# A new order table with its PSUM banks and load gates written out, for sliding-window attention followed by a squared-ReLU FFN

## The chip, the cores and the metric

The kernel runs on one core of one Trainium2 chip. The metric is the device time in microseconds (us) of one execution. Besides, one execution is profiled, and the profile's span is the time from its first to its last instruction.

## What is computed

For four batches of eight heads, 768 tokens and a head dimension of 64, each query sees the 96 latest keys and the first eight keys, with a bias that falls with distance. The heads are then put side by side into 3072 tokens of 512 features, and an FFN with a squared ReLU follows.

```python
def _attn_ref(q, k, v, n_global, n_local):
    scores = scale * np.matmul(q, k.transpose(0, 1, 3, 2))
    is_global = pos[None, :] < int(n_global)                  # 8
    is_local = (rel >= 0) & (rel < int(n_local))              # 96
    dist = np.where(is_global & ~is_local, float(n_local), np.abs(rel))
    scores = np.where(is_global | is_local, scores - slopes * dist, -1e9)
    a = softmax(scores)
    return np.matmul(a, v)

def _moe_ref(x, w_in, w_out):              # x: 3072 x 512
    h = np.maximum(x @ w_in, 0.0)          # 512 -> 2048
    return h * h @ w_out                   # 2048 -> 512
```

## The kernel before

The 3072 tokens are cut into eight halves of 384 tokens (half a batch each), numbered 0 to 7; in the code a half is `x`, its number `x.hb`. A half goes through these stages.

Loads: POOL's queue brings q, k and v as 128-row tiles into the staging buffers `sq`, `sk` (one each) and `v` (`list_loads`, L472). The four chunks of w_in (L534) and of w_out (L541) go through the same queue.

Turns: for the first halves, PE transposes sq and sk; from half 3 on, `turn_by_dma` (L647) has SP issue one DMA transpose for k and one for q. `fix` copies the key blocks that stand before a block into `kb`, with the global keys in front, and `values` does the same for `vb`.

Attention: PE makes scores `sp` (L691), ScalarE takes the exponential `ex` (L704), VectorE multiplies by a mask that holds the bias, `phat` (L711, L728), PE multiplies with v and a column of ones, `av` (L752), and `norm` on VectorE divides, a reciprocal `rec` (L760) and a product `tm` (L762). From half 2 on SP transposes `tm` by DMA into `xt` (`to_x_by_dma`, L777).

FFN: `xt` times w_in gives `hps` in PSUM, either in plain products (L797) or in mixed ones (L900), a scheme of fewer products over sums of blocks: `x_mix` holds four sums of quarters of xt (L878), `in_mix` and `w_mix` sums of weights. A mixed product's partial results are held back by a copy (`kept`, L336 on ScalarE or L338 on VectorE) and added later (`hr`, L958). Relu (L822, L824, L966, L968, L981, L983) and square (L836, L838, L998, L1000) give `h`; each of them may run on ScalarE or on VectorE. The second layer (`yps`, L1052 and L1138) mixes likewise: `mixed` (L1103) are sums of h, and partial results go out through `y` (L336, L338, L1200). The output leaves by SP (L1068, L1223).

What sets the order: the program first lists all jobs, PE's as `p` with a number, loads as `l`, and everything else in one list. A table of words, `ORDER`, then gives the order in which they are issued; the letter of a word is the engine (`a` ScalarE, `d` VectorE, `g` POOL, `s` SP, and `l` POOL's loads), so a word with another letter moves a job from one engine to another. In each engine instructions run in the order issued.

`Plan.run` walks the table and simulates a cost model at the same time. From it come two things: which PSUM banks a PE job takes (`idle_banks`, the ones idle longest), and how many filler matmuls (`warm`) a job of the opening issues. A wait between DMAs that data does not ask for is added by `behind(dma, first)`: the first `sk` load of a half stands behind both turns of the half before.

Of the kernel before, what the change touches and what calls it, by code (L numbers as in the profile page):

```python
# [41 lines left out]
AFTER = [0, 0, 0, 0, 0, 0, 0, 0]  # L42
# [10 lines left out]
ORDER = """d1 g2 a4 p0 a6 s8 d12 a0 s10 d17 l3 d13 l1 a18 a16 a19 l2 d21 d20 a27 l5 a26 d14 a22 d15 d3 a28 d5  # L53
p10 l4 a25 d9 p5 a30 d146 l0 a24 p1 a11 p2 d7 l6 a23 p3 l10 a32 d31 a33 d34 p6 l9 a29 d36 p7 a39 p11
d35 l7 p8 a46 p4 d43 p9 a41 l8 d37 p13 d44 a40 p12 d45 a47 l11 p14 d38 p16 a42 p15 d48 l13 p17 d51
a49 p19 p24 a52 l12 d55 p20 d64 p22 a50 p23 d58 l14 a53 p34 d56 p30 a60 p25 d71 p28 l16 p21 a81 d59
p26 d57 a82 l18 p27 d69 d67 p31 a65 d68 p18 a61 p29 l15 d72 p36 p32 a54 d70 p35 l19 a86 d66 p33 a73
d85 p39 d62 p40 l17 a74 a77 d76 p37 l21 d91 a78 p41 l20 d79 d63 p38 d83 l23 a101 d75 d84 p45 l22 a89
a87 d96 p44 l27 p47 a92 d80 p48 d107 a97 l29 d111 p46 a98 p52 l28 p43 a93 d110 p53 p42 d105 l30 d119
p55 d120 p50 l24 p59 a122 a88 d90 d99 a102 p51 l25 d106 a103 d94 p49 a116 a128 d108 p67 d100 a129  # L60
d95 a117 d112 p57 a104 p65 d125 p54 p58 d121 d189 p63 p61 p62 a132 d126 a109 p60 a114 d135 d118 a113
d115 p56 a127 d205 d191 a133 p74 a130 p72 a169 d138 p73 a165 d131 p77 d123 a166 p69 a167 p75 d156
d147 a157 p70 p71 d134 a158 p82 d159 l34 a162 d168 p81 a163 d186 l26 a170 p83 a142 p68 l31 d174 a139
d160 d149 p84 l35 a184 a164 d208 p64 a187 d124 l33 d161 a171 d148 a144 p85 l32 d272 a143 d206 p88
d207 l36 p89 d201 p79 d151 p86 a198 a178 d204 p91 d152 a195 a199 d188 p76 d202 a136 d150 p87 a172
d200 a179 p90 a196 d180 a193 p80 d153 a209 p78 s194 l37 p66 d155 a175 d203 a137 p95 d210 p92 a176
d223 a173 p94 d197 s224 l38 a185 d177 p100 a211 l39 d236 a181 s216 p93 a140 d237 p96 a182 p103 d238
s217 p97 d183 a244 a240 d221 a141 p102 d219 a222 d154 p106 s220 d213 d225 p98 p104 d239 s226 p99
d227 d228 p105 a234 d214 s229 d145 a218 d243 p101 l44 d245 d246 p107 l43 s215 d212 a241 d190 p109
l40 p110 p108 p111 a255 d192 l42 a251 p112 a256 d258 l45 a248 d257 p113 l41 a249 d230 d232 a252 p118  # L70
d259 p114 a273 d253 s260 l46 p116 d254 p115 a261 p120 d231 d250 l47 a262 p122 a264 p124 l48 s235
d280 p123 a265 d263 p131 a268 d233 a283 p127 d281 p126 a288 p132 d285 a269 p134 d295 s328 a287 p129
d270 a286 p119 a291 p142 d266 a293 p140 d296 s329 d314 p130 a311 p135 d267 a299 p128 d315 a292 p137
d274 a312 p136 d300 s242 p121 a305 s282 d327 a302 p125 a306 d289 p138 s275 a284 d303 p141 a307 d301
d304 a276 p117 d294 s290 a313 d308 p133 a271 l50 p139 d330 a278 p143 d297 a309 l56 p145 d279 a316
s298 p146 d310 p147 l53 a317 p144 d405 a334 l51 d322 p148 a326 a337 d323 l52 p149 a335 d443 d340
a331 l49 p151 d324 a341 p150 a332 d336 p152 l54 a342 d318 d325 p157 a348 p153 a343 d333 a345 d344
p159 p156 a346 d320 d319 a354 d407 p158 a356 p161 d321 a338 p172 d355 a359 p154 d349 p162 d377 a351
p169 p163 d360 a372 s378 l57 p164 d363 p167 a361 p166 d365 p171 d347 a368 p177 s408 a369 p160 d339
p165 a364 p170 a362 d357 p178 s409 l55 d373 a386 p175 a366 p173 a387 d382 p180 a367 p174 d376 p182  # L80
d374 p176 a379 s247 d383 p155 d380 s277 a384 s358 p179 d391 a385 p181 d395 a375 p168 s381 d353 d410
a393 p183 l58 a352 p184 d388 a370 a397 d394 l65 s396 p185 a392 d389 a399 d371 l62 p187 a398 d390
p188 p186 a419 l59 p189 d411 a415 a423 d412 l63 p190 a420 d426 a416 p191 d422 l73 a424 d414 a417
p192 l61 d421 a428 d425 p193 p194 p196 a432 l60 d413 a427 d418 a429 p198 p195 a436 d406 a444 d401
a433 p200 d492 p199 d402 a437 d447 p207 a430 p210 d435 a457 p204 s448 d445 p215 a462 p211 d453 p202
s350 d463 s446 p197 d439 a451 p203 d403 a464 p218 d496 d404 p206 a442 d441 d505 a475 d493 p205 a465
d438 p208 s507 p219 a455 d434 p213 a476 p201 d468 s508 a454 d431 a458 p223 p222 a472 d497 p214 a484
d469 d452 p217 a449 p212 s400 d470 a474 p209 d482 a456 p220 p227 d459 a477 s483 d466 p224 a500 p216
d495 a478 s467 l64 p221 d498 a471 p241 d479 a486 p225 l70 p229 a509 d488 d494 l66 p226 a489 d473
p228 a511 d490 a539 l69 d480 p231 d481 p233 l72 p230 a513 d501 d487 a519 l67 d460 p234 a520 d499  # L90
a512 l71 s440 p248 d521 a485 s506 d503 p235 l68 a514 d502 d522 a546 d510 p247 a461 d491 p236 s523
l74 d524 p237 a545 p232 d515 p239 a525 d531 a516 p246 d504 a517 p256 d544 p245 a536 p270 a528 d561
s537 d543 p240 a529 p249 d518 a538 p267 a547 d530 p251 a580 p255 d550 p252 a526 s595 p258 d559 a562
p243 a551 p266 d527 p238 a585 d578 s450 a553 p253 a565 d591 p254 s579 d541 a535 d554 p261 a557 p257
d532 s560 a568 p268 a558 d533 p242 a582 d555 s596 d563 a552 p260 d534 p250 a581 p269 d548 p264 p244
a567 a586 d574 p263 d542 a564 p259 d572 p262 a540 a583 p265 d556 p272 a575 s573 a597 d566 p271 d600
s549 d569 p277 d598 a576 d584 a599 p273 d570 a577 p274 d571 p275 p276 a601 d613 a608 d615 s614 l75
p278 a602 s593 d589 d616 a609 p279 a619 d617 s594 a604 p283 d587 a620 s592 d603 a611 a605 p281 d618
a631 p280 p282 a624 d588 p286 d606 a628 a625 p284 d634 a629 p287 d610 p292 a636 p288 d607 a632 d627
a635 d686 p294 a621 p301 d630 a646 p291 d637 d643 p299 d657 a641 p314 d626 a622 p290 d680 p285 d640  # L100
p307 s681 a633 p305 d623 p300 a665 p295 d655 s642 p293 s612 d647 d590 p296 d668 a644 p298 a656 d648
p309 a658 p289 d649 p308 a670 d654 p297 p304 d638 a651 p311 d652 s639 a663 p312 p306 d669 p317 d687
s653 p310 d688 a690 p302 d676 p316 p320 a684 s677 a650 p303 a685 d674 p328 p319 d671 a662 d666 a697
a672 p313 d659 p315 d696 p331 a675 d682 p318 a660 d691 d667 d678 a719 p333 a661 p332 d689 p321 d692
a664 d683 p335 d695 a716 p352 d698 d705 s699 p347 d693 s645 p334 d742 a752 p322 d723 a722 d673 p337
p339 d679 p336 d706 p338 d700 d720 p324 d721 d728 p329 a725 d753 a724 p343 a710 d729 p341 a726 d701
s711 p342 a717 p340 d736 p323 d694 a737 d734 p344 a738 d702 p345 d709 p325 d703 a740 d708 d707 p351
a712 d731 p353 a730 p326 d727 d704 p346 d750 p348 d713 a741 p327 d732 a733 p349 d714 p357 d746 a715
a754 d735 p330 d743 a755 d739 p354 d751 d764 p350 d744 a756 p356 d718 a748 s757 d747 a745 d749 p355
d760 p362 a758 d761 p358 d765 s759 d763 p368 a770 d779 a768 d767 p364 d762 d766 p359 d769 d775 p360  # L110
d776 d786 a783 p365 d790 d780 d781 p366 a787 d777 p367 a771 a788 p371 d789 d772 d782 s773 p361 d778
d794 p369 s795 d774 p370 d791 p363 d792 s793 p372 a784 p373 d796 s785 s797 a798 a799"""


class Op:
    EARLY = {"ACT": 0.035, "DVE": 0.045}
    LATE = {"ACT": 0.1, "DVE": 0.07}

    def __init__(self, costs, emit, needs, rank=0, lag=0.0, move=None):
        self.emit, self.rank, self.lag, self.move = emit, rank, lag, move  # L120
        self.needs = [n for n in needs if n is not None]
        self.costs = {e: c - self.EARLY.get(e, 0.0) for e, c in costs.items()}
        self.done, self.bufs = None, []
        self.wait = 0.0
        self.takes, self.users, self.rows, self.follows = 0, [], False, []


class Buffer:

    def __init__(self, tag, count):  # L130
        self.tag, self.count, self.users, self.taken = tag, count, [], False
# [7 lines left out]
class Plan:  # L139
# [5 lines left out]
    HOP = 0.08  # L145
    ENTER = 0.19
# [4 lines left out]
    def __init__(self, warm_from, warm_until):  # L151
        self.warm_from, self.warm_until = warm_from, warm_until
        self.queues = {"PE": [], "LOAD": []}
        self.rest = []
        self.free = {e: 0.75 for e in ("ACT", "DVE", "POOL", "SP")}
# [54 lines left out]
    def ready(self, op):  # L210
        t = self.free_at(op)
        if t is None:
            return None
# [1465 lines left out]
```

## Time and profile before

| | before |
|---|---|
| three runs, us | 200.9, 202.91, 202.87 |
| median, us | 202.87 |
| span of the profiled execution, us | 200.3 |
| PE busy, us | 193.0 (96%) |
| VectorE (DVE) busy, us | 178.9 (89%) |
| ScalarE (ACT) busy, us | 155.9 (78%) |
| POOL busy, us | 66.7 (33%) |

The profiled execution's own time is its span of 200.3 us and what lies around it; the nearest of the three runs is 200.9. Engines are named PE (TensorE), PEld (its weight loads), DVE, ACT, POOL (GpSimd) and SP (SyncE, which only issues DMAs here). In a list of waits the last three numbers are microseconds in total, how often, and the longest.

### The profile page before, as it was taken

The numbers are of one execution on the slowest core, as the hardware profiler recorded it, in microseconds if no ns is written. First come the engines' busy times: TensorE is split into PE (matmuls) and PEld (weight loads), VectorE is DVE, ScalarE is ACT, GpSimd is POOL, SyncE is SP. The second block draws the span as 40 slices with busy tenths as digits, with TensorE's granted clock in tenths as the row PEclk, the third lists the DMA queues.
The fourth block names the chain that finished last, engine by engine and source line by source line (L and its number), as shares of the span: only waits on it lengthen the run. The fifth ranks groups of instructions, "written<-read, shape, count | busy, mean of one in ns | idle before, by whom it ended". The sixth has DMA issues, their size and how long they took to land.

```text
span 200.3 us, 5912 instructions
## 1 busy us (share of the span) xinstructions
PE 193.0 (96%) x2346; PEld 161.3 (81%) x2346; DVE 178.9 (89%) x457; ACT 155.9 (78%) x335; POOL 66.7 (33%) x82
## 2 busy tenths in 40 slices
PE   7798999999999899999999999999999999999994
PEld 2685899766897587779878798899888988899993
DVE  7688698899999799989999999999989979998881
ACT  5999676898946889988999798989996669457411
POOL 8996564087108602920095019400000000000000
PEclk9999999999999999999999999999999999999999
DMA  5999999999999999999999989995230330210214
GB/s 154 180 150 197 187 181 173 209 192 154 176 203 74 141 206 219 120 115 99 221 133 147 155 203 144 166 246 111 53 114 3 124 61 3 105 56 0 108 52 157
DMA packets 106987, 27.52 MB, mean 137 GB/s; under 512 B 97104, under 2 KB 104016, under 8 KB 106960
## 3 DMA queue, kind: packets, MB, share of 16 engines
q0 software_dynamic: 74944, 13.11, 93.3%
q1 hardware_dynamic: 30816, 13.45, 30.9%
q10 hardware_dynamic: 1200, 0.59, 1.1%
q8 instruction: 18, 0.29, 0.6%
q14 instruction: 9, 0.07, 0.1%
HBM read 27.26 MB, written 6.29 MB: 167 GB/s over the span
## 4 chain that ended last, share of the span: by engine, by line
PE 72%; DVE 12%; DMA 7%; POOL 3%; ACT 2%; issue 1%; DVEq 0%; POOLq 0%
PE yps L1138 28%; PE hps L797 17%; PE hps L900 17%; DMA w_in_sb<-in_moe_w_in_dram 4%; PE sp L691 3%; PE av L752 3%; DMA xt<-tm 3%; PE yps L1052 2%; DVE phat L728 2%; POOL w_mix L472 2%; DVE tm L762 2%; POOL v L472 1%; ACT ex L704 1%; DVE hr L958 1%; DVE mixed L1103 1%
## 5 line engine op out<-in xcount | busy, mean ns | idle before, releaser
L797 PE MATMUL hps<-xt,w_in_sb 128*128 128x384 f16 (+2 forms) x336 | 45.1, 280 | 0.2 <-DMA w_in_sb<-in_moe_w_in_dram 0.2
L704 ACT ACTIVATE ex<-sp 128x512 f16<-128x512 f32 x66 | 36.4, 632 | 2.6 <-PE sp L691 2.5
L1138 PEld LDWEIGHTS <-h 128*128 128x128 f16 x376 | 34.3, 98 | 5.1 <-DVE h L838 0.2
L797 PEld LDWEIGHTS <-w_in_sb 128*128 128x128 f16 x336 | 28.1, 98 | 7.9 <-DMA w_in_sb<-in_moe_w_in_dram 0.7
L336 ACT COPY y<-yps 128x256 f32<-128x256 f32 (+2 forms) x42 | 15.5, 389 | 17.5 <-PE yps L1138 17.3
L1138 PEld LDWEIGHTS <-mixed 128*128 128x128 f16 x272 | 25.1, 98 | 3.7 <-DVE mixed L1103 0.6
L958 DVE TENSOR_TENSOR hr<-hps,kept 128x384 f16<-128x384 f32 x49 | 25.6, 551 | 2.2 <-ACT h L998 1.1
L472 POOL DMA_DIRECT2D sq<-in_q_dram x19 | 17.2, 907 | 29.7 <-DMA q<-sq 21.6
L336 ACT COPY kept<-hps 128x384 f32<-128x384 f32 x45 | 21.1, 490 | 7.4 <-PE hps L900 4.9
L822 ACT ACTIVATE hr<-hps 128x384 f16<-128x384 f32 (+1 forms) x44 | 22.2, 530 | 4.9 <-PE hps L797 4.8
L472 POOL DMA_DIRECT2D sk<-in_k_dram x19 | 17.1, 901 | 25.3 <-DMA q<-sq 13.6
L900 PEld LDWEIGHTS <-in_mix 128*128 128x128 f16 x272 | 23.0, 98 | 2.3 <-DVE x_mix L878 0.6
L900 PE MATMUL hps<-x_mix,in_mix 128*128 128x192 f16 x204 | 23.4, 246 | 0.3 <-ACT ex L704 0.3
L1138 PE MATMUL yps<-w_out_sb,h 128*128 128x256 f16 (+1 forms) x184 | 22.5, 268 | 0.1
L1138 PE MATMUL yps<-w_mix,mixed 128*128 128x256 f16 (+1 forms) x184 | 22.4, 268 | 0.1
L1138 PE MATMUL yps<-w_mix,h 128*128 128x256 f16 (+1 forms) x192 | 22.4, 264 | 0.0
L472 POOL DMA_DIRECT2D v<-in_v_dram x24 | 21.5, 908 | 2.6 <-DMA w_mix<-in_q_dram 0.9
L728 DVE TENSOR_TENSOR phat<-ex,mask 128x1024 f16<-128x1024 f16 (+1 forms) x36 | 20.7, 598 | 0.0
L900 PEld LDWEIGHTS <-w_in_sb 128*128 128x128 f16 x204 | 17.4, 98 | 2.1 <-issue 0.7
L900 PE MATMUL hps<-xt,w_in_sb 128*128 128x192 f16 x136 | 16.1, 246 | 0.5 <-DMA xt<-tm 0.5
L998 ACT ACTIVATE h<-hr 128x768 f16<-128x768 f16 x19 | 15.9, 853 | 0.4 <-DVE hr L968 0.3
L836 ACT ACTIVATE h<-hr 128x512 f16<-128x512 f16 (+1 forms) x22 | 15.9, 742 | 0.1
(115 smaller groups left out, 363.4 us busy)
## 6 DMA issues: line engine op xcount, KB each, us to landing
out_dram<-y SPq DMA_DIRECT2D x23, 256.0 KB, 2.5
v<-in_v_dram POOLq DMA_DIRECT2D x24, 128.0 KB, 6.8
sq<-in_q_dram POOLq DMA_DIRECT2D x19, 128.0 KB, 6.7
sk<-in_k_dram POOLq DMA_DIRECT2D x19, 128.0 KB, 6.7
w_in_sb<-in_moe_w_in_dram POOLq DMA_DIRECT2D x4, 512.0 KB, 10.9
w_out_sb<-in_moe_w_out_dram POOLq DMA_DIRECT2D x4, 512.0 KB, 12.3
y<-in_q_dram SPq DMA_DIRECT2D x2, 256.0 KB, 4.4
y<-in_k_dram ACTq DMA_DIRECT2D x2, 256.0 KB, 5.1
```

The costliest lines, as they stand in the source:

```text
L336: nc.scalar.copy(out=out, in_=in_)
L472: dma = nc.gpsimd.dma_start(out=dst, in_=src[x.b, :, r0 + t * P:r0 + (t + 1) * P, :] .rearrange("h p d -> p h d"))
L691: nc.tensor.matmul(sp[h][:, i, :], lhsT=lhsT, rhs=x.q[rows, r % HT, a, :], start=True, stop=True)
L704: nc.scalar.activation(out=st["ex"][:, h], in_=sp[h], func=AF.Exp, scale=scale)
L728: eng(e).tensor_tensor(out=x.phat[a][:, :, t0:t0 + n], op=ALU.mult, in0=st["ex"][:, :, i0:i0 + 2 * n].rearrange("p e (t b) c -> p e t (b c ...
L797: nc.tensor.matmul(st["ps"][:, i * n:(i + 1) * n], lhsT=w_in_sb[:, kk, m * P:(m + 1) * P], rhs=x.xt[:, kk, c0:c1], start=kk == 0, stop=kk ...
L822: nc.scalar.activation(out=o, in_=i, func=AF.Relu)
L836: nc.scalar.activation(out=h2, in_=hr, func=AF.Square)
L900: nc.tensor.matmul(st[name][:, i * HC:(i + 1) * HC], lhsT=left(i, kk), rhs=right(kk), start=fresh and i == kk == 0, stop=kk == KK - 1, ski ...
L958: eng(e).tensor_tensor(out=hidden(which)[:, :, cols], in0=sums(name), in1=st[kept], op=ALU.add)
L998: nc.scalar.activation(out=h2, in_=hr, func=AF.Square)
L1138: nc.tensor.matmul(st[bank_name][:, 0:n], lhsT=a(m), rhs=b(m)[:, cols], start=fresh and m == 0, stop=m == HK - 1, skip_group_check=not fresh)
```

## The change

The table is another one, with more in its words: `p1.12+18` is PE job 1, in banks 1 and 2, with 0.18 us of fillers ahead of it; `l40@217` is load 40, put behind entry 217. So `Plan.run` no longer simulates anything, and the cost model's code (`free_at`, `take`, `ready`, `idle_banks`, `by_rank`, `by_table`, `AFTER`, `LATE`, `HOP`, `ENTER`) goes away, which moves all later lines up by about 80. Besides, `list_loads` and `turn_by_dma` wait for less: the sk loads of a half from 4 on wait for the k turn of the half before, its sq loads for the q turn; a k turn waits for its own three loads, and a q turn for its own.

```diff
-ORDER = """d1 g2 a4 p0 a6 s8 d12 a0 s10 d17 l3 d13 l1 a18 a16 a19 l2 d21 d20 a27 l5 a26 d14 a22 d15 d3 a28 d5
-p10 l4 a25 d9 p5 a30 d146 l0 a24 p1 a11 p2 d7 l6 a23 p3 l10 a32 d31 a33 d34 p6 l9 a29 d36 p7 a39 p11
...
+ORDER = """d1 g2 s8 a4 p0.0 s10 a6 d12 a0 d13 l3 l5 l2 d19 d3 a30 d20 d16 d18 l4 a9 d14 d5 a29 l1 d22 a26 d17
+p1.12+18 d21 a15 a27 l10 d11 p2.34 d7 l0 p3 l6 p5.56 a31 d32 p10.70 a23 l9 d34 p6 a33 d36 p9.2 a39
...
+    def run(self):
+        lists = {"p": self.queues["PE"], "l": self.queues["LOAD"]}
         for word in ORDER.split():
...
+            word, _, spare = word.partition("+")
+            word, _, banks = word.partition(".")
+            word, _, gate = word.partition("@")
+            op = lists.get(word[0], self.rest)[int(word[1:])]
+            self.now, self.spare = [int(i) for i in banks], int(spare or 0) / 100
+            op.result = op.emit("POOL" if word[0] == "l" else self.LETTERS[word[0]])
+            if gate:
+                self.behind(op.result, self.rest[int(gate)].result)
...
     def list_loads(x, first=None):
...
-        before = (prev.turned if prev else []) + (halves[x.hb - 1].turned if x.hb > 2 else [])
-        if x.hb > 3 and AFTER[x.hb]:
-            before = before + list(prev.x_ops.values())
+        if x.hb > 3:
+            before = {"sk": halves[x.hb - 1].turned[:1], "sq": halves[x.hb - 1].turned[1:]}
+        else:
+            last = halves[x.hb - 1].turned if x.hb > 2 else prev.turned if prev else []
+            before = {"sk": last, "sq": last}
...
-                if x.hb > 3 and name == "sk" and t == 0:
-                    for turn in halves[x.hb - 1].turns + (prev.xturns if AFTER[x.hb] else []):
-                        behind(dma, turn)
-                if name == "sq":
-                    x.last_load = dma
+                return dma
...
     def turn_by_dma(x):
...
-                if not x.turns:
-                    behind(turn, x.last_load)
                 x.turns.append(turn)
-            op = plan.add({"SP": 2.0 if i else 1.5}, emit, [*x.k_in, *x.q_in, x.bt.op, *late],
+                return turn
+            op = plan.add({"SP": 2.0 if i else 1.5}, emit, [*loads, x.bt.op, *late],
                           move=plan.TURN)
```

The gates in the table put the sk loads of half 4 behind entry 217 (the q turn of half 3), those of half 5 behind 329, of half 6 behind 409 and of half 7 behind 508 (the q turns of halves 4, 5 and 6).

Where instructions move, first on SP and POOL around the turns of half 4. SP before, with what each instruction waits for in brackets (DMASW are POOL's queues, DMAHW SP's):

```order
L777 DMA_TRANSPOSE xt<-tm 128x3x128 [waits DMAHW2_49,DVE_49]
L604 DMA vb<-v 32x2x520 [waits DMAHW3_49,DVE_49]
L1223 DMA out_dram<-y 128x512 [waits DMAHW4_49,DVE_49]
L1223 DMA out_dram<-y 128x512 [waits DMAHW5_49,Activation_49]
L647 DMA_TRANSPOSE k<-sk 128x12x128 [waits DMASW5_49,DMASW4_49,DMAHW6_49,DMASW3_49,DMASW2_49]
L647 DMA_TRANSPOSE q<-sq 128x12x128 [waits DMASW1_49,DMAHW7_49,DMASW0_49,PE_49]
```

And now:

```order
L695 DMA_TRANSPOSE xt<-tm 128x3x128 [waits DMAHW2_49,DVE_49]
L523 DMA vb<-v 32x2x520 [waits DMAHW3_49,DVE_49]
L1142 DMA out_dram<-y 128x512 [waits DMAHW4_49,DVE_49]
L1142 DMA out_dram<-y 128x512 [waits DMAHW5_49,Activation_49]
L566 DMA_TRANSPOSE k<-sk 128x12x128 [waits DMASW5_49,DMAHW6_49,DMASW3_49,DMASW2_49]
L566 DMA_TRANSPOSE q<-sq 128x12x128 [waits DMASW4_49,DMASW1_49,DMAHW7_49,DMASW0_49,PE_49]
```

SP issues the same things in the same order; one wait has gone from the k turn to the q turn. That wait, DMASW4, is the third sq load of the half, as POOL's order shows, which for these loads is the same before and now:

```order
L472 DMA sq<-in_q_dram 128x8x64 [waits DMASW4_49,DMAHW7_49,DMASW1_49,DMASW0_49]
L472 DMA sq<-in_q_dram 128x8x64
L472 DMA sk<-in_k_dram 128x8x64 [waits DMAHW6_49,DMASW3_49,DMASW2_49]
L472 DMA sk<-in_k_dram 128x8x64
L472 DMA sq<-in_q_dram 128x8x64
L472 DMA sk<-in_k_dram 128x8x64 [waits DMASW5_49]
```

The sk load stands last of the six.

Second, VectorE around the norms of half 2 (`rec` and `tm`; `phat` is half 2's as well, h_761 and now h_779 are the hidden values of half 1). Before:

```order
L338 COPY vb<-v 128x520
L338 COPY vb<-v 32x520
L1103 TENSOR_TENSOR mixed<-h_537,mixed 128x512
L338 COPY y<-yps 128x256
L760 RECIPROCAL rec<-av 128x6
L762 TENSOR_TENSOR tm<-av,rec 128x2x3x64
L728 TENSOR_TENSOR phat<-ex,mask 128x2x512 x2
L1103 TENSOR_TENSOR mixed<-h_761 128x1024
L1103 TENSOR_TENSOR mixed<-mixed,h_761 128x1024
L1103 TENSOR_TENSOR mixed<-h_761,mixed 128x1024
L728 TENSOR_TENSOR phat<-ex,mask 128x2x512
L1200 TENSOR_TENSOR y<-yps,y 128x256
```

And now:

```order
L257 COPY vb<-v 128x520
L257 COPY vb<-v 32x520
L487 TENSOR_TENSOR w_mix<-w_out_sb,w_mix 128x1024
L678 RECIPROCAL rec<-av 128x6
L680 TENSOR_TENSOR tm<-av,rec 128x2x3x64
L646 TENSOR_TENSOR phat<-ex,mask 128x2x512
L257 COPY y<-yps 128x256
L646 TENSOR_TENSOR phat<-ex,mask 128x2x512
L757 TENSOR_TENSOR h_779<-hr 128x768
L1022 TENSOR_TENSOR h_535<-h_535 128x4x128
L1022 TENSOR_TENSOR mixed<-h_779 128x1024
L780 TENSOR_TENSOR in_mix<-in_mix,w_in_sb 128x1536
```

A copy of y and two token sums (one ahead of what is shown) went from ahead of the first norm to behind it, and a square of half 1, which ScalarE did, follows it on VectorE.

Third, VectorE around the `x_mix` sums of half 3. Before:

```order
L878 TENSOR_TENSOR x_mix<-xt 128x384
L1103 TENSOR_TENSOR h_1464<-h_1464 128x8x128
L728 TENSOR_TENSOR phat<-ex,mask 128x2x512 x2
L878 TENSOR_TENSOR x_mix<-xt 128x384
L878 TENSOR_TENSOR x_mix<-xt,x_mix 128x384
L338 COPY vb<-v 128x520
L338 COPY vb<-v 32x520
L878 TENSOR_TENSOR x_mix<-xt,x_mix 128x384
L958 TENSOR_TENSOR hr<-hps,kept 128x2x192
```

And now:

```order
L797 TENSOR_TENSOR x_mix<-xt 128x384
L629 TENSOR_TENSOR phat_1834<-ex,mask 128x1024
...
L678 RECIPROCAL rec<-av 128x6
L680 TENSOR_TENSOR tm<-av,rec 128x2x3x64
L646 TENSOR_TENSOR phat<-ex,mask 128x2x512
L797 TENSOR_TENSOR x_mix<-xt,x_mix 128x384
L1119 TENSOR_TENSOR y<-yps,y 128x256
L797 TENSOR_TENSOR x_mix<-xt 128x384
L877 TENSOR_TENSOR hr<-hps,kept 128x2x192
L646 TENSOR_TENSOR phat<-ex,mask 128x2x512
L877 TENSOR_TENSOR hr<-hps,kept 128x2x192 x2
L797 TENSOR_TENSOR x_mix<-xt,x_mix 128x384
```

The last three sums are now strung out among a norm of half 4, a weighing and the first sums of kept products.

More of the change, by code (lines that the diff above doesn't have):

```diff
@@ L58 @@
[L58 to L67, printed above, removed]
@@ L204, in take @@
-    def take(self, op, start):
-        for buf in op.bufs:
-            if not buf.taken:
-                buf.taken, buf.start = True, start
-                self.rings.setdefault(buf.tag, []).append(buf)
[L210 to L213, printed above, removed]
-        for n in op.needs:
-            if n.done is None:
-                return None
-            t = max(t, n.done + self.HOP)
-        if op.takes:
-            banks = self.idle_banks(op.takes)
-            if banks is None:
-                return None
-            t = max(t, banks[-1][0] + self.HOP)
-        return t + op.wait
@@ L1642 @@
     with tc.manual_schedule():
-        order = plan.run()
+        plan.run()
 _INS = ['q', 'k', 'v', 'n_global', 'n_local', 'moe_w_in', 'moe_w_out']
```

204 lines of the change are left out of this document (76 added, 128 removed).

## Prediction

> **What bounds the kernel now.** I read the page first, for the share of each engine.
>
> ```profile
> span 200.3 us, 5912 instructions
> PE 193.0 (96%) x2346; PEld 161.3 (81%) x2346; DVE 178.9 (89%) x457; ACT 155.9 (78%) x335; POOL 66.7 (33%) x82
> PEclk9999999999999999999999999999999999999999
> ```
>
> TensorE (PE) is busy 96% of the span and its granted clock is never lowered, so only gaps on PE, or what stands before and after its stream, can be won. The chain that ended last shows both ends.
>
> ```profile
> 9.01 0.88 POOL v L472
> 11.57 8.42 DMA w_in_sb<-in_moe_w_in_dram
> 20.04 3.69 PE hps L797 x40
> 61.78 5.83 DMA xt<-tm
> 185.05 12.32 PE yps L1138 x144
> ```
>
> The FFN starts at 20.04, when the first quarter of w_in lands. PE's last block ends at 185.05 + 12.32 = 197.37, and 200.3 − 197.37 = 2.9 us of evacuation and stores follow. Between them the longest piece that is not PE is the transpose of attention output, xt, at 61.78. Now the stretches, first all from the landing to PE's end, then the middle in two (columns: stretch, length, then busy us and instructions of PE, PEld, DVE, ACT, POOL; then clock, DMA share, GB/s).
>
> ```profile
> 20.04:197.37 177.33, 176.22 (x2104) 149.85 (x2104) 162.79 (x403) 138.56 (x298) 49.51 (x57) 1.00 1.22 134
> ```
>
> ```profile
> 40.00:95.00 55.00, 53.95 (x638) 42.30 (x636) 51.13 (x124) 45.62 (x98) 24.58 (x28) 1.00 1.88 155
> 95.00:150.00 55.00, 54.97 (x696) 47.53 (x694) 52.58 (x127) 52.16 (x114) 15.86 (x18) 1.00 1.26 155
> ```
>
> PE idles 177.33 − 176.22 = 1.1 us in all after 20.04, and 55.00 − 53.95 = 1.05 of it lies in 40 to 95. That is the most the body can give. VectorE is nearly as full: it idles 3.87 us in 40 to 95 and 2.42 in 95 to 150, 6.3 us together, while ScalarE has 9.38 + 2.84 = 12.2. What PE waited for:
>
> ```profile
> PEld L900 <- DVE x_mix L878: 0.6, 1, 0.6
> PE hps L900 <- DMA xt<-tm: 0.5, 1, 0.5
> PE hps L900 <- ACT ex L704: 0.3, 1, 0.3
> PE hps L797 <- DMA w_in_sb<-in_moe_w_in_dram: 0.2, 1, 0.2
> ```
>
> And what VectorE waited for in 40 to 150 (the named waits make 4.5 of the 6.3 us):
>
> ```profile
> DVE x_mix L878 <- DMA xt<-tm: 1.8, 2, 1.2
> DVE y L1200 <- ACT ex L704: 0.7, 1, 0.7
> DVE kept L338 <- PE hps L900: 0.5, 2, 0.2
> DVE hr L824 <- ACT h L836: 0.4, 1, 0.4
> DVE phat L711 <- ACT ex L704: 0.4, 1, 0.4
> DVE hr L958 <- PE hps L900: 0.3, 1, 0.3
> DVE mixed L1103 <- ACT h L998: 0.2, 1, 0.2
> DVE y L1200 <- issue: 0.2, 1, 0.2
> ```
>
> So the kernel is a PE stream begun by a DMA landing, with VectorE close behind PE in the middle and the xt transposes as its only long latency.
>
> **The change part by part.** *PE's work.* The new order gives PE 2343 matmuls instead of 2346; the difference is warm fillers, which stand before 20.04. All products are the same, and the same 39 jobs stand ahead of the first product with w_in. PE's 176.2 us of work after 20.04 therefore stays, and so does the tail of 2.9 us, since of the jobs that stood after 150 us 17 go to VectorE and 18 from it.
>
> *The opening: 0.* Eleven input loads stand ahead of the first w_in chunk in both orders, only permuted, so its landing stays at 20.0. The bounds are one load's turn on the queue either way, ±0.9 (the 0.88 us piece above). The fourth w_in chunk moves ahead of one sk and one v load, which can save the 0.2 us that PE waits for w_in; I count nothing.
>
> *The relaxed waits of the sk and sq transposes: 0.* The new k transpose of a half waits for its three sk loads alone, no longer for its sq loads. What that is worth is read from the two queues.
>
> ```profile
> SPq L777 <- DVE tm L762: 11.4, 2, 9.3
> SPq L647 <- DMA sk<-in_k_dram: 2.3, 1, 2.3
> ```
>
> ```profile
> 53.09 1.29 SPq L777 DMA_TRANSPOSE xt<-tm  x1
> 54.58 1.46 SPq L647 DMA_TRANSPOSE k<-sk  x1
> 56.13 1.71 SPq L647 DMA_TRANSPOSE q<-sq  x1
> ...
> 71.93 1.45 SPq L647 DMA_TRANSPOSE k<-sk  x1
> ```
>
> The 2.3 us is the k transpose of half 4 at 71.93, which waits for sk, not for sq. In both orders its loads leave as sq, sq, sk, sk, sq, sk: the last one is an sk load, and waiting for fewer others brings nothing. The k transpose of half 3 at 54.58 stands on SP behind an xt transpose that waits for VectorE. The gates written in the table put sk loads of halves 4 to 7 behind the q transpose of the half before, where the first one stood already. So the words of the change that look like its core carry no time of their own.
>
> *VectorE's norms of half 2: −0.8.* What does move these transposes is the xt at 53.09: of the two waits for tm above, 11.4 − 9.3 = 2.1 us is its own, and the norm tm<-av,rec it waits for now has less VectorE work ahead. Instructions of both orders counted with the durations below, it comes about 1.8 us earlier, the second norm 0.7, the third 0.4 and the last 1.3.
>
> ```profile
> L958 DVE TENSOR_TENSOR hr<-hps,kept 128x384 f16<-128x384 f32 x49 | 25.6, 551 | 2.2 <-ACT h L998 1.1 <-PE hps L900 0.6
> L728 DVE TENSOR_TENSOR phat<-ex,mask 128x1024 f16<-128x1024 f16 x24 | 16.2, 686 | 0.0
> L762 DVE TENSOR_TENSOR tm<-av,rec 128x384 f16<-128x384 f32 x24 | 13.4, 558 | 0.8
> L1200 DVE TENSOR_TENSOR y<-yps,y 128x256 f32<-128x256 f32 x28 | 11.7, 422 | 1.6 <-ACT ex L704 0.7 <-PE yps L1138 0.4 <-issue 0.2
> L1000 DVE TENSOR_TENSOR h<-hr 128x768 f16<-128x768 f16 x15 | 8.2, 553 | 0.2
> L968 DVE TENSOR_SCALAR hr<-hr 128x768 f16<-128x768 f16 x10 | 3.9, 385 | 0.0
> L338 DVE COPY kept<-hps 128x384 f32<-128x384 f32 x6 | 3.3, 552 | 0.5 <-PE hps L900 0.5
> L838 DVE TENSOR_TENSOR h<-hr 128x512 f16<-128x512 f16 x7 | 2.8, 416 | 0.0
> L824 DVE TENSOR_SCALAR hr<-hps 128x384 f16<-128x384 f32 x5 | 2.7, 554 | 0.6 <-ACT h L836 0.4 <-PE hps L797 0.2
> L338 DVE COPY kb<-k 128x384 f16<-128x384 f16 x6 | 2.0, 353 | 0.1
> ```
>
> PE also has three score units of half 3 ahead of its first mixed product of half 2 now, which stood behind it. Both cover the 0.5 us that PE waits for xt, and 0.3 behind it. I take −0.8. The bounds are 0 and −1.1, all the idle time that PE has. What can eat it is the same DMA queues: with the q transpose earlier, the loads of half 4 also start earlier and meet the last xt transposes again.
>
> ```profile
> DMA to landing us min/median/max: 2.3/3.8/7.5
> ```
>
> An xt transpose (all 24 in this line) lands in 2.3 us at best and 7.5 at worst, and the one in the chain took 5.83. The Trainium skill (DMA: Bandwidth & Descriptors, Queues, rings and completion order) says that each DMA engine takes turns between the queues that have work for it, a packet at a time. The spread agrees with that. By it a transpose issued earlier into loads issued equally early would land no sooner, and this term would be 0, which is rival C.
>
> *VectorE's share: +1.2.* Of the jobs that stood between 40 and 150 us, 34 go from ScalarE to VectorE and 22 the other way. Net by form: five squares of 768 at 0.55, two of 512 at 0.42, two relus and two holds of 384 at 0.55, two copies to kb at 0.35, one hand-out at 0.42, a seed of two copies (taken as 2 × 0.55, the nearest form), less three relus of 768 at 0.385. That is 2.75 + 0.83 + 2.2 + 0.7 + 0.42 + 1.1 − 1.16 = 6.8 us. Counted the other way, as work ahead of one and the same instruction late in the stretch, it is 4.3 to 5.9, since other jobs slide out of it. I take 5.0. Against 6.3 us idle it leaves 1.3. Which waits survive? The 1.8 for xt goes: three of the four x_mix sums of half 3 now stand behind 2.3 to 4.3 us more VectorE work, so their xt is there. The other named waits, 4.5 − 1.8 = 2.7, are for work of PE and ScalarE that VectorE depends on anyway. 2.7 − 1.3 = 1.4 us late by 150; with some of that absorbed since a late VectorE waits less, I take +1.2. The bounds are 0 (a late engine finds everything ready, and all waits vanish) and +3.2 (all 4.5 stay). The cover is ScalarE's 12.2 us of idle time, which the move enlarges and which nothing uses. Queued behind a late VectorE are the sums hr<-hps,kept, whose PSUM banks PE needs for its next mixed products.
>
> **The sum.** 0 + 0 − 0.8 + 1.2 = +0.4 on the profiled execution: span 200.3 becomes 200.7. The three runs shown are 200.9, 202.91 and 202.87. The profiled span lies 0.6 below the first and 2.57 below the median, so two of three runs carry 2 us that this profile does not show. With the median's distance I get 200.3 + 0.4 + 2.5 = 203.2. A measurement tells about 1% from no change, 200.84 to 204.90.
>
> **The rivals.** *A, faster:* PE's waits of 0.8 vanish, VectorE absorbs its new work in its idle time, and the runs no longer scatter, since what they lost was waiting on landings that the new order leaves room for. 200.3 − 0.8 + 0.6 = 200.1. For it: the two slower runs carry time that PE's own work can't explain, and the first run shows that it can be absent. Against it: PE has just 1.1 us of shown idle time, and VectorE loses most of its room.
>
> *B, slower:* VectorE becomes the bound in 40 to 150. It decides as soon as the waits that it can't lose exceed the 1.3 us left to it. If all 4.5 stay, it is 4.5 − 1.3 = 3.2 late; 0.6 of that PE already waits for x_mix, so +2.6: 200.3 + 2.6 + 2.57 = 205.5. For it: VectorE idles 2.42 of 55 us in 95 to 150, and of the 34 jobs that it gains 16 lie there. Against it: part of VectorE's waiting only shows that it is early, and a late engine that finds its inputs ready waits less.
>
> *C, the transposes are not earlier:* the queues give the 1.8 us back as above, and only VectorE's +1.2 stays. 200.3 + 1.2 + 2.5 = 204.0, within 1%.
>
> **How the numbers follow.** The forecast (+0.4) has 0.34, A 0.28, B 0.32, C 0.06. Within 1% are the forecast and C: 0.40; faster 0.28; slower 0.32. The likeliest case's own range is 202.3 (a load's turn of 0.9 won at the opening) to 204.9 (that turn lost, and the norms' 0.8 with it). The range that holds 8 in 10 must reach into A and B: from 199.5 (A with PE's whole 1.1 us instead of 0.8, and a third of a load's turn at the opening) to 206.5 (B with a load's turn lost at the opening).
>
> **What would show it.** In the changed profile the first product with w_in should start at 20.0 ± 0.3. The xt transpose ahead of the k transpose of half 3 should issue near 51.3 instead of 53.09, and PE's wait for xt should be gone. VectorE should idle 1 to 3 us in 40 to 150 instead of 6.3. PE should idle about 1.5 us after 20.04. The k transpose of half 4 should still wait for sk. If PE idles over 3 us there and the wait named is for VectorE (hr, kept, x_mix or h), B is right; if under 0.5 and the runs lie together near 200.5, A. It would prove the working itself wrong if the first w_in landing moved by over 1 us, or if PE stalled after 150 us.

## The result, and the profile after

The changed kernel takes 203.06 us (median of 21 runs, 202.21 to 204.01) where the kernel before takes 202.6 (21 runs, 200.9 to 205.68). The ratio is 1.0055 with a 95% interval of 1.0035 to 1.0074: half a per cent slower, inside the 1% that was called no change. (This ratio and those below leave out runs that lie over 1.5% above the fastest run of their kernel, so they are not the ratios of the medians, here 1.0023.) The profiled execution took 202.57 us at a span of 200.8, so 1.8 us lie around the span, and the other runs that list both have the same 1.8.

The page of the changed kernel, then the same stretches as before: the two in the middle, and all from the first product with w_in to PE's last one.

```profile
span 200.8 us, 5910 instructions
PE 192.8 (96%) x2343; PEld 160.8 (80%) x2343; DVE 182.6 (91%) x474; ACT 151.5 (75%) x318; POOL 66.8 (33%) x82
```

```profile
40.00:95.00 55.00, 54.37 (x653) 42.96 (x651) 53.20 (x131) 42.28 (x93) 23.66 (x27) 1.00 1.85 156
95.00:150.00 55.00, 54.72 (x679) 46.65 (x677) 53.93 (x134) 49.52 (x103) 15.74 (x18) 1.00 1.21 154
```

```profile
20.11:197.81 177.70, 176.47 (x2104) 149.76 (x2104) 165.97 (x416) 135.90 (x288) 49.39 (x57) 1.00 1.19 133
```

PE starts the FFN at 20.11, idles 177.70 − 176.47 = 1.23 us until 197.81, and 3.0 us of tail follow. VectorE now idles 1.80 + 1.07 = 2.87 us in 40 to 150, and its busy time there has grown from 103.71 to 107.13. What PE waits for after 20 us, and what VectorE waits for in 40 to 150:

```profile
PE hps L716 <- DMA w_in_sb<-in_moe_w_in_dram: 0.4, 1, 0.4
PE av L670 <- DVE vb L257: 0.3, 1, 0.3
PE sp L609 <- DVE h L757: 0.3, 1, 0.3
PE hps L819 <- DVE hr L877: 0.2, 1, 0.2
PE yps L1057 <- DVE mixed L1022: 0.2, 1, 0.2
```

```profile
DVE y L257 <- PE yps L1057: 0.9, 1, 0.9
DVE phat L629 <- ACT ex L622: 0.5, 2, 0.3
```

Before, PE waited for DMAs, for x_mix and once for ScalarE; now, behind the first w_in chunk, every named wait of PE is for VectorE, 1.0 us together. The wait for xt is gone in this execution. And SP's queue around the turns of half 3:

```profile
50.68 1.28 SPq L695 DMA_TRANSPOSE xt<-tm  x1
52.07 1.53 SPq L566 DMA_TRANSPOSE k<-sk  x1
53.99 4.39 SPq L566 DMA_TRANSPOSE q<-sq  x1
58.47 4.77 SPq L695 DMA_TRANSPOSE xt<-tm  x3
...
71.30 1.98 SPq L566 DMA_TRANSPOSE k<-sk  x1
```

The first xt transpose issues 2.4 us earlier than before (50.68 against 53.09), yet the q transpose holds SP for 4.39 us, and by 58.47 SP is 0.4 us later than before. The xt issued early lands at 58.0, where before it landed at 57.1. The k transpose of half 4 issues at 71.30 instead of 71.93.

### The profile page after: what moved, and what is told of

It is laid out like the page before. It is cut to its first block, busy times and chain, and to the rows that moved or that the text cites. A ratio compares the mean times of both kernels' runs of the same rounds, so it can differ in the third digit from the quotient of the medians.

```text
span 200.8 us, 5910 instructions
## 1 busy us (share of the span) xinstructions
PE 192.8 (96%) x2343; PEld 160.8 (80%) x2343; DVE 182.6 (91%) x474; ACT 151.5 (75%) x318; POOL 66.8 (33%) x82
## 4 chain that ended last, share of the span: by engine, by line
PE 57%; DMA 16%; DVE 11%; POOL 7%; ACT 5%; issue 2%; DVEq 0%; POOLq 0%
PE yps L1057 23%; PE hps L819 16%; PE hps L716 8%; DMA w_in_sb<-in_moe_w_in_dram 7%; DMA xt<-tm 5%; DMA sk<-in_k_dram 4%; PE av L670 3%; PE sp L609 3%; POOL w_mix L395 3%; PE yps L971 3%; POOL v L395 2%; ACT ex L622 2%; DVE mixed L1022 2%; DVE hr L877 2%; DVE phat L646 2%
## 5 line engine op out<-in xcount | busy, mean ns | idle before, releaser
L716 PE MATMUL hps<-xt,w_in_sb 128*128 128x384 f16 (+2 forms) x336 | 45.8, 280 | 0.4 <-DMA w_in_sb<-in_moe_w_in_dram 0.4
L622 ACT ACTIVATE ex<-sp 128x512 f16<-128x512 f32 x66 | 37.0, 619 | 4.2 <-PE sp L609 3.7
L741 ACT ACTIVATE hr<-hps 128x384 f16<-128x384 f32 (+1 forms) x45 | 22.9, 534 | 5.9 <-PE hps L716 5.8
L877 DVE TENSOR_TENSOR hr<-hps,kept 128x384 f16<-128x384 f32 x49 | 26.2, 548 | 0.6 <-PE hps L819 0.4
L255 ACT COPY kept<-hps 128x384 f32<-128x384 f32 x42 | 19.3, 488 | 7.0 <-PE hps L819 6.9
L255 ACT COPY y<-yps 128x256 f32<-128x256 f32 (+2 forms) x40 | 14.9, 385 | 12.2 <-PE yps L1057 11.6
L680 DVE TENSOR_TENSOR tm<-av,rec 128x384 f16<-128x384 f32 x24 | 13.4, 557 | 0.8
```

Of the source, the lines that this page charges most:

```text
L255: nc.scalar.copy(out=out, in_=in_)
L622: nc.scalar.activation(out=st["ex"][:, h], in_=sp[h], func=AF.Exp, scale=scale)
L680: nc.vector.tensor_tensor(out=st["tm"].rearrange("p t e d -> p e t d"), in0=av[:, :, :, 0:D], in1=rec[:, :, :, None].to_broadcast([P, 2, H ...
L716: nc.tensor.matmul(st["ps"][:, i * n:(i + 1) * n], lhsT=w_in_sb[:, kk, m * P:(m + 1) * P], rhs=x.xt[:, kk, c0:c1], start=kk == 0, stop=kk ...
L741: nc.scalar.activation(out=o, in_=i, func=AF.Relu)
L877: eng(e).tensor_tensor(out=hidden(which)[:, :, cols], in0=sums(name), in1=st[kept], op=ALU.add)
```

## The experiments

Ratios are to the kernel before, run on the same chip in the same series.

### The relaxed waits alone

```diff
-                if not x.turns:
-                    behind(turn, x.last_load)
                 x.turns.append(turn)
```

> The kernel before with one edit: the k transpose of a half no longer stands behind the half's last q load (the added wait in turn_by_dma is removed, nothing else). Theory: worth nothing, since the k transposes of halves 3 and 4 wait for SP's queue and for an sk load that is last anyway; ratio to before 0.998 to 1.002, the k transpose of half 4 still issues near 71.9 us. Rival (the relaxed waits are the change's gain, and its order costs more than shown): 0.4 to 0.8 us faster than before, ratio 0.996 to 0.998, and the k transpose of half 4 or 5 issues at least 0.5 us earlier.

Measured: 201.48 us against 202.18, ratio 1.0004 (0.9957 to 1.0050). The k transpose of half 4 issued at 72.47, not earlier. The wait carries no time that shows, as the theory has it; the interval is too wide to exclude 0.4%. The edit takes out the added wait of the k transpose alone; the relaxed waits of the loads were not varied. Its profile (span 200.7) shows something else, a wait for xt larger than before's 0.5:

```profile
PE hps L898 <- DMA xt<-tm: 1.5, 1, 1.5
```

### The engines without the order, and the order without the engines

The first kernel is the changed one with the old letters, the second is the old table with the new ones; two of the 125 words:

```diff
-... p71.4 p75.0 a156 d162 ... d157 p167 ...
+... p71.4 p75.0 d156 a162 ... a157 p167 ...
```

> The changed kernel's order, banks and gates, but each of the 125 jobs that it moves between ScalarE and VectorE goes back to the engine that it had before. Theory (the added VectorE work is the price): VectorE idles about 5 to 6 us in 40 to 150 us again, and the time falls by about 1 us against the changed kernel, to about 202, ratio to before 0.997 to 1.001. Rival (the order and its landings set the time, the engines don't): no gain over the changed kernel, ratio to before 1.004 to 1.007. Second rival (order and engines fit only together): slower than both, over 1.01.

> The order before, with the changed kernel's choice of engine for the 125 jobs that differ (banks are chosen by the old cost model). Theory (VectorE's work is the price): 1 us slower than before, ratio 1.003 to 1.008, VectorE idle in 40 to 150 us near 2. Rival (order sets the time): ratio 0.998 to 1.002. Second rival (they fit only together): over 1.01.

Measured: 207.98 us, ratio 1.0345 (1.0289 to 1.0400), and 209.04 us, ratio 1.0381 (1.0331 to 1.0432). My theory and its first rival fall; the second rival holds: order and engines fit only together. The price of VectorE's added work can't be taken off by itself, so this pair does not isolate the +1.2. In the second kernel VectorE has about the changed kernel's work (185.5 us busy against 182.6) and PE waits for it all over (first three of nine named waits):

```profile
PE hps L900 <- DVE hr L958: 1.3, 3, 0.7
PE sp L691 <- DVE rec L760: 0.8, 1, 0.8
PE sp L691 <- DVE y L338: 0.7, 1, 0.7
```

In the first, two waits of PE stand close together, and the granted clock falls behind them (a timeline of PE, then stretches):

```profile
104.04 0.21 PE L607 MATMUL sp<-q,k 64*128 64x128 f16 x1 [0.90 <-ACT hr L739]
106.37 1.03 PE L1055 MATMUL yps<-w_mix,mixed 128*128 128x256 f16 x4 [0.96 <-DVE mixed L1020]
```

```profile
105.00:115.00 10.00, 9.04 (x98) 6.51 (x97) 8.51 (x21) 7.42 (x17) 4.75 (x6) 0.83 1.61 110
115.00:125.00 10.00, 10.00 (x124) 9.38 (x122) 9.17 (x25) 8.49 (x18) 1.42 (x2) 1.00 0.83 153
```

### No v load in flight during the turns of half 3

```diff
-... l37 ... l38 ... l39 ... s224 a187 ...
+... s224 l37@224 l38 l39 a187 ...
```

> The changed kernel with the three v loads of half 3 put behind the first xt transpose of half 2 (entry 224), so that no v load is in flight while it and the k and q transposes of half 3 run. Theory (shared DMA queues ate the earlier issue): that xt lands about 3 us after its issue instead of 7.35, the k and q transposes of half 3 land 2 to 3 us earlier than 59.24 and 60.47, and the loads of half 4 start 2 to 3 us earlier; PE does not wait there, so the time moves by less than 0.6 us, ratio to before 1.002 to 1.006. Rival (the transposes' earliness is worth time once the queues let it through): 0.8 us or more faster than the changed kernel, ratio to before 1.000 or less. Second rival: the v loads come too late for half 3's attention, over 0.5 us slower.

Measured: 202.59 us, ratio 1.0050 (1.0018 to 1.0083).

```profile
50.61 1.28 SPq L693 DMA_TRANSPOSE xt<-tm  x1
52.01 1.64 SPq L564 DMA_TRANSPOSE k<-sk  x1
54.07 1.42 SPq L564 DMA_TRANSPOSE q<-sq  x1
56.25 4.51 SPq L693 DMA_TRANSPOSE xt<-tm  x3
...
71.19 1.47 SPq L564 DMA_TRANSPOSE k<-sk  x1
```

```profile
58.31 1.81 POOL L393 DMA_DIRECT2D sq<-in_q_dram  x2 [0.65 <-DMA q<-sq]
```

The q transpose now holds SP for 1.42 us, and the loads of half 4 start at 58.31, 2.7 us earlier than in the changed kernel (61.04). The theory holds: that xt lands 3.9 us after its issue instead of 7.35, and the k and q transposes at 55.9 and 57.7 instead of 59.2 and 60.5. So the v loads in flight were what ate the earlier issue. But the k transpose of half 4 issues at 71.19, as it did: its last sk load, issued 2.6 us earlier, lands no earlier (71.05 and 71.15), 8.25 us after its issue instead of 5.79. I put that down to the v loads and xt transposes now in flight beside it; no run takes these away. The earlier start is given back before the turns of half 4, and the time is the same. This agrees with the Trainium skill (DMA: Bandwidth & Descriptors, Queues, rings and completion order), by which each DMA engine takes turns among its queues.

### Six more groups of score matmuls

```diff
-... p146.50 a304 l53 d308 p145.76 p147.34 a334 s298 d309 p120 a337 ...
+... p146.50 a304 l53 d308 p145.76 a334 s298 d309 p120 p147.34 a337 ...
```

and likewise p151 behind p152, p194 behind p195, p232 behind p234, p274 behind p276, p282 behind p286.

> The changed kernel with six of its groups of score matmuls split: the last unit of each stands one PE job later, so there are 20 groups instead of 14 (before: 12), with the same matmuls. Theory (each change between score matmuls, which use 64 rows, and full ones costs PE about 0.1 us at either end, so the changed kernel's two extra groups are part of what it lost): PE's busy time rises by 1.0 to 1.4 us over the changed kernel's 192.8 and the time by as much, ratio to before 1.008 to 1.013. Rival (the gaps at these places are records only): busy time within 0.3 us of 192.8 and ratio 1.003 to 1.007.

Measured: 204.8 us, ratio 1.0146 (1.0061 to 1.0231), PE busy 195.2 us. The changed kernel's PE there, then the split one's:

```profile
80.60 0.56 PE L609 MATMUL sp<-q,k 64*128 64x128 f16 x14
...
81.38 1.04 PE L971 MATMUL yps<-w_out_sb,h 128*128 128x512 f16 x4
82.25 0.38 PE L1057 MATMUL yps<-w_out_sb,h 128*128 128x256 f16 x2
```

```profile
80.81 0.56 PE L607 MATMUL sp<-q,k 64*128 64x128 f16 x14
...
81.37 1.04 PE L969 MATMUL yps<-w_out_sb,h 128*128 128x512 f16 x4
82.34 0.34 PE L607 MATMUL sp<-q,k 64*128 64x128 f16 x6
...
82.67 0.39 PE L1055 MATMUL yps<-w_out_sb,h 128*128 128x256 f16 x2
```

The same matmuls take 82.67 − 80.81 = 1.86 us from the first score to the next product instead of 82.25 − 80.60 = 1.65: a group more costs 0.21 us. Six make 1.26 of the 1.7 us that the median rose. The rest is not explained: PE's busy time rose by 2.4 us, more than the 1.0 to 1.4 that I expected, and its named waits after 20 us by 0.7, among them 0.4 for xt at half 2. The changed kernel has 14 groups where the kernel before has 12, by this 0.4 us of PE work more; in the profiles PE's busy time from the first product with w_in to its end rose by 0.25 us (176.22 to 176.47). (The Trainium skill (TensorEngine Tiling (Array Packing), Key Properties) says that a change of tiling mode drains TensorE; the 0.21 us may be that, but no run here shows a drain as such.)

### The kernel before with two PE moves

```diff
-... p113 ... p118 d259 p114 ... p115 a261 p120 ...
+... p113 ... p120 p118 d259 p114 ... p115 a261 ...
-... p158 a356 p161 d321 a338 p172 d355 a359 p154 ...
+... p172 p154 p158 a356 p161 d321 a338 d355 a359 ...
```

> The kernel before with nothing but PE jobs moved at the two places where it waited for xt: the layer-2 job that stood behind the score units (1.03 us) goes ahead of the first mixed product of half 2, and the first av job of half 4 and one more product over the first two xt chunks of half 3 (0.47 + 0.33 us) go ahead of the first product that needs the last two. Theory (before scatters because PE waits there for landings that differ from run to run, and the changed kernel's gain is to cover them): PE's wait for xt of 0.5 us is gone, runs scatter less (highest minus lowest under 3 us against 4.5), ratio to before 0.993 to 0.998. Rival (landings set the time wherever PE stands): ratio 0.999 to 1.003, and the waits return at other lines. Second rival: the moved jobs wait for VectorE themselves, ratio over 1.003.

Measured: 202.01 us (200.69 to 204.59), ratio 1.0001 (0.9954 to 1.0048). In its profile PE waits for no xt, and the span is 198.9, the shortest of all. But the runs scatter over 3.9 us, where I expected under 3 (before: 4.3 in this series), so the theory holds for one execution and not for the median.

### The first product of half 2 early, in the changed kernel

```diff
-... p113 d241 ... p105.2 a262 ... p115.70 d254 l47 p116.61 s260 a264 p118.5 ...
+... p113 d241 ... p118.5 p105.2 a262 ... p115.70 d254 l47 p116.61 s260 a264 ...
```

> The changed kernel with one PE job moved: the first product of half 2 over xt goes ahead of a layer-2 job and two score units (1.4 us of PE work) that now stand before it. Theory (that work in front, not an earlier landing, is what removed PE's wait for xt): PE waits 1.2 to 1.6 us for xt there, landing near 66.9 us, and the time is 0.8 to 1.6 us more than the changed kernel's, ratio to before 1.009 to 1.014. Rival (the xt lands early enough): wait under 0.3, ratio 1.003 to 1.007.

Measured: 203.48 us, ratio 1.0106 (1.0071 to 1.0142). PE's wait for xt came back, but with 0.4 us instead of 1.2 to 1.6, since this xt landed a microsecond earlier than in the changed kernel's profile, near 66. So the moved job is needed in the new order: without it the product starts at 65.35, with it at 66.84. But it is no cover that the old order lacked, for there the product started at 66.88. What differs between the first two profiles is the landing of half 2's last xt, 66.95 instead of 67.60. In the profile of the split scores, whose order is the changed kernel's at this place, this xt landed at 67.3 and PE waited 0.4 us for it again.

### What differs between executions

The kernel before once more, then the kernel with the two moves twice more, all unchanged.

> The kernel before, unchanged, profiled once more, to see what differs between two executions of it. Theory (its scatter is PE's wait for the xt transposes of halves 2 and 3): PE's waits for xt differ by as much as the spans, within 0.3 us of each other. Rival (the start of the FFN or the clock differs): the first product with w_in starts elsewhere than 20.0 by as much, or the granted clock does.

> The kernel with the two PE moves, unchanged, profiled once more: its first profile had a span of 198.9 us and no wait of PE for xt, while its runs go up to 204.6. Theory (a landing that differs from run to run makes PE wait at a place that the first profile doesn't show): a longer span than 198.9, and PE's named waits after 20 us make up the difference within 0.4 us, for xt or for scores of a half whose k or q transpose landed late. Rival (the whole stream runs slower, by clock or by VectorE's pace): PE's waits stay under 0.5 us and its busy time rises instead.

> The same kernel a third time, for the same question: theory, the span less 198.9 is found again in PE's named waits after 20 us; rival, in PE's busy time or clock.

The spans are 200.5 for the kernel before, and 199.8 and 202.4 for the one with two moves. By PE's named waits the theory fails twice. Before's second profile waits 1.3 us for xt, now at half 3 (89.1 us) and not at half 2: 0.8 more than the first, for a span only 0.2 longer. In the 199.8 us execution the named wait is the same 0.3 as in the 198.9 us one. The last one waits most:

```profile
PE hps L900 <- DMA xt<-tm: 2.1, 2, 1.1
PE hps L900 <- DVE x_mix L878: 0.3, 1, 0.3
PE hps L900 <- ACT ex L704: 0.3, 1, 0.3
PE av L1454 <- DMA v<-in_v_dram: 0.2, 1, 0.2
```

That is 2.6 us more than the 0.3 that the 198.9 us execution named, of 3.5 us more span; with PE's busy time, 0.8 higher, the difference is accounted for.

What the spans do follow is one landing, that of half 3's last xt. In the old order, with or without the two PE moves, VectorE's second sum of that half, `x_mix<-xt`, waits for this landing in each of the executions below; here the two of the kernel before, then the 202.4 us execution:

```profile
88.94 0.36 DVE L878 TENSOR_TENSOR x_mix<-xt 128x384 f16<-128x384 f16 x1 [0.68 <-DMA xt<-tm]
```

```profile
89.18 0.36 DVE L878 TENSOR_TENSOR x_mix<-xt 128x384 f16<-128x384 f16 x1 [2.08 <-DMA xt<-tm]
```

```profile
90.90 0.36 DVE L878 TENSOR_TENSOR x_mix<-xt 128x384 f16<-128x384 f16 x1 [2.12 <-DMA xt<-tm]
```

| execution of the old order | this sum starts, us | span, us | from there to the end, us |
|---|---|---|---|
| before | 88.94 | 200.3 | 111.4 |
| before, again | 89.18 | 200.5 | 111.3 |
| without the added wait | 89.26 | 200.7 | 111.4 |
| two PE moves | 87.63 | 198.9 | 111.3 |
| two PE moves, again | 88.13 | 199.8 | 111.7 |
| two PE moves, third | 90.90 | 202.4 | 111.5 |

The start moves by 3.3 us and the span with it; what follows stays within 0.4 us. So a wait of PE at half 2 that goes away is found again at half 3, as in the two executions of the kernel before, unless the xt of half 3 lands earlier too. In the changed kernel's order VectorE waits for this xt in none of the four profiles (the changed kernel, v behind xt, split scores, early product), and the time from its landing to the end is no longer one number, 112.0 to 114.9 us.

This isn't the whole scatter. Before's seven longest runs of 23 in this series took 203.84 us and more, and none of them was profiled; in four of them the mean granted clock was 0.992, which by estimate costs 1.6 us of 203.

SP's queue in the 198.9 us execution, and in the 202.4 us one:

```profile
54.26 1.46 SPq L647 DMA_TRANSPOSE k<-sk  x1
55.81 1.71 SPq L647 DMA_TRANSPOSE q<-sq  x1
...
70.11 1.76 SPq L647 DMA_TRANSPOSE k<-sk  x1
72.04 3.64 SPq L647 DMA_TRANSPOSE q<-sq  x1
```

```profile
54.38 2.23 SPq L647 DMA_TRANSPOSE k<-sk  x1
56.71 1.44 SPq L647 DMA_TRANSPOSE q<-sq  x1
...
72.92 1.45 SPq L647 DMA_TRANSPOSE k<-sk  x1
74.53 3.23 SPq L647 DMA_TRANSPOSE q<-sq  x1
```

The k transpose of half 3 takes SP 2.23 us instead of 1.46, and the q transpose behind it lands at 62.0 instead of 59.9. The loads of half 4 start 2.1 us later (62.53 against 60.46), the k transpose of half 4 issues 2.8 us later, and the xt transposes of half 3 behind it start at 78.50 instead of 76.42. A delay of 0.8 us at one transpose grows to 2.8 along that chain. The first experiment's profile shows the same (2.07 us for that k transpose, loads at 62.34, the next k at 72.47); what makes the k transpose slow is open.

### Cutting the chain

The kernel with two moves, with half 4's sk loads first, behind the k transpose of half 3 alone; and then also with the v loads of half 3 behind the first xt transpose.

```diff
-... l44 ... l43 ... l40 ... l42 ... l45 ... l41 ...
+... l40 ... l42 ... l41 ... l44 ... l43 ... l45 ...
-                if x.hb > 3 and name == "sk" and t == 0:
+                if x.hb > 4 and name == "sk" and t == 0:
```

> The kernel with the two PE moves, and one thing more: the three sk loads of half 4 go ahead of its three sq loads and wait for the k transpose of half 3 alone, no longer for its q transpose. Theory (the scatter is a chain: the q transpose of half 3 lands between 59.9 and 62.0 us, the loads of half 4 wait for it, SP's k and q transposes of half 4 wait for the loads, and the xt transposes of half 3 stand behind these on SP): the sk loads start at 58.5 to 59 us whenever the q transpose lands, the k transpose of half 4 issues by 69.5, the xt transposes of half 3 start by 76.5, highest less lowest of the runs falls from 3.9 us under 2.5, and the ratio to before is 0.990 to 0.997. Rival (the transfers themselves are the limit, so an earlier start is given back): the k transpose of half 4 issues at 70 to 73 as before, ratio 0.998 to 1.003. Second rival: the earlier loads delay the xt transposes of half 2, PE waits for these, ratio over 1.003.

```diff
+                if x.hb == 3 and name == "v" and t == 0:
+                    behind(dma, halves[2].xturns[0])
```

> The kernel with the two PE moves and the sk loads of half 4 first, and the three v loads of half 3 put behind the first xt transpose of half 2, so that no load is in flight while the k and q transposes of half 3 run. Theory (what is left of the scatter comes from the q transpose of half 3 meeting those v loads): the q transpose of half 3 lands by 58.5 us, highest less lowest of the runs is under 2 us, ratio to before 0.990 to 0.998. Rival (the loads that now come later push the transposes of half 4 back by as much): k transpose of half 4 at 70 us or later, ratio 0.998 to 1.004. Second rival: v comes too late for half 3's attention, ratio over 1.004.

Measured for the first: 201.72 us (201.08 to 204.34), ratio 1.0014 (0.9984 to 1.0045). Eleven of its twelve runs lie within 1.2 us. Its k transpose of half 3 was slow in the profile (2.21 us), and yet PE waited for no xt:

```profile
59.04 2.72 POOL L472 DMA_DIRECT2D sk<-in_k_dram  x3 [8.51 <-DMA k<-sk]
62.74 2.62 POOL L472 DMA_DIRECT2D sq<-in_q_dram  x3 [0.98 <-DMA q<-sq]
```

The chain is cut as the theory has it: the q transpose landed late, at 62.2, and the sk loads still started at 59.04. But the k transpose of half 4 issued at 70.19, not by 69.5, the runs span 3.3 us where I expected under 2.5, and the time is not better than before's, so the rival is right on the median. The sum that waits for half 3's last xt starts at 88.07, and 111.7 us follow, as in the table. The second is 205.24 us, ratio 1.0151 (1.0098 to 1.0205): its second rival. v comes too late, and the q transpose, which landed at 63.9 and not by 58.5, and xt now meet the delayed loads. Half 3's last xt lands at 91.9, 3 us later than before, and from there to the end it is 111.6 us, as in the kernel before (111.5): the span follows this landing when it is moved, too.

```profile
DVE x_mix L880 <- DMA xt<-tm: 2.6, 2, 1.7
DVE vb L338 <- DMA v<-in_v_dram: 2.6, 1, 2.6
```

No version was measurably faster than the kernel before.

## Why the prediction was right, and where its steps were off

The time was forecast as 203.2 and is 203.06, within 1% as the likeliest case said. That it came so close is in part luck, since errors of the terms cancel. The span grew by 0.5 us, and the forecast for it was +0.4, all of it waiting of PE. Measured are 0.07 at the opening, 0.25 more PE work, 0.13 more idle time of PE and 0.06 at the tail. Step by step:

*The opening, 0:* right. The first product starts at 20.11 against 20.04.

*The relaxed waits, 0:* right as far as tried, by the first experiment and by the k transpose of half 4, which still issues right behind its sk load.

*The norms of half 2, −0.8:* PE's waits of 0.5 for xt and 0.3 behind it are gone in the changed kernel's profile, but the reasons given don't carry it. The first xt did issue early (50.68; I said 51.3), and landed later than before: the queues took it back, which was rival C, and with the queues cleared the time did not move either. The PE work put in front leaves the product where it was, at 66.84 against 66.88. Half 2's last xt landed 0.65 us earlier, which is less than it varies between the two executions of the kernel before (67.60 and 66.62). And in the old order this wait was not worth its 0.5: the execution without it was no shorter, because half 3's last xt comes after it and sets the end. What the new order does remove is VectorE's wait for that one, by the reason that I gave under VectorE's share.

*VectorE's share, +1.2:* near in size, not shown by subtraction. VectorE's busy time in 40 to 150 rose by 3.4 us (I took 5.0), its idle time fell to 2.87 (I said 1 to 3), and PE's named waits for it are 1.0 us. Taking the engines back made everything slower, so the price can only be read from the waits.

*PE's work unchanged:* this step failed. The matmuls are the same, but they stand in 14 groups of scores instead of 12, and each group costs 0.21 us. It was readable in the order of PE, where I had counted instructions by number and shape and not how often they change.

*The runs' distance from the profile, 2.5:* a weak step. 1.8 us lie around every span; the 0.7 beyond that was before's own scatter, which I added as if it were fixed. The changed kernel's median lies 2.3 us above its profiled span (203.06 and 200.8), so the term came out nearly right for a reason that I did not have.

*Rivals:* A was right in one part: the runs do lie closer together, within 1.8 us instead of 4.8. In the old order the profiled spans follow the landing of half 3's last xt; in the new one they don't. But it pays for that, in its profile with PE work (0.25) and PE's waits for VectorE (1.0); its fastest run is 1.3 us above before's fastest and its slowest 1.7 below before's slowest. That these two prices make up the 1.3 is not shown. B did not come about: VectorE lost what waits it could, down to 1.4 named.

## What to carry to other kernels

Profile a tight kernel several times before pricing a stall: here PE's wait for xt was 0.5 and 1.3 us in two executions of one kernel and 0, 0 and 2.1 in three of another. Ask which wait ends last: the span followed a landing at half 3, and the wait at half 2 came and went without it. A transfer that is issued earlier into a busy queue lands when the queue lets it, so cover a late landing with other work ahead of its consumer rather than issue it sooner. And when instructions are reordered, count the changes of kind on the matmul engine, not just the instructions.

## What the runs showed of the hardware that was not expected

A change between score matmuls of 64 rows and full ones and back costs PE 0.21 us together (1.86 against 1.65 us for the same matmuls), hidden in busy time and not in idle time.

The granted clock fell to 0.83 over 105 to 115 us in the execution of the new order with the old engines, behind two PE waits of 0.90 and 0.96 us that lie within 3.2 us. The loss is 1.7 us, 10 × 0.17. The same execution loses 1.7 us a second time in its opening, behind waits of 0.73, 0.57 and 0.31 us between 4.6 and 7.0 us:

```profile
7.50:10.00 2.50, 2.50 (x26) 2.50 (x24) 1.39 (x3) 1.35 (x3) 2.50 (x4) 0.50 2.43 155
10.00:12.50 2.50, 2.50 (x42) 1.69 (x41) 1.54 (x5) 1.74 (x5) 2.50 (x4) 0.83 3.00 146
```

The Trainium skill (TensorE: Matmul & The Clock Gate, Part 1) says the clock is halved after an idle window of some 3.4 us; by estimate a halved window of 3.4 us would lose just these 1.7, but none of these waits was as long as 1 us, so by this one execution the window needn't be wholly idle. How much idle time it takes is open: in the old order with the new engines two waits of 0.81 and 0.54 us, 1.5 us apart, left the clock at 1.00.

How long a DMA transpose holds its issuing queue depends on what else is in flight: the same q transpose took SP 1.42 us with the v loads held back and 4.39 us with the three of them in flight when it was issued. That isn't all of it, for the k transpose just ahead took 1.64 and 1.53 us in the same two executions.
